# Attention stage: each step's reciprocals written 64 times by GpSimd and turned beside the last keys of the next step

## The chip, the cores and the metric

The kernel runs on one core of one Trainium2 chip. The metric is the device time of one execution in microseconds (us); less is better. TensorE (PE) multiplies matrices out of SBUF into PSUM, its weight loads are listed as PEld. VectorE (DVE) and ScalarE (ACT) work on SBUF and PSUM, GpSimd (POOL) on SBUF, and SyncE (SP) issues the DMAs. Each engine executes its own list in the order in which the program gave it; semaphores tie the lists together.

## The reference, cut to what matters

```python
scores = scale * q @ k.T + bias                # B=2, H=8, S=576, D=64; bias from a small MLP of positions
attn = np.exp(scores - scores.max(-1))
attn = attn / (attn.sum(-1) + 1e-9)
x = attn @ v                                   # -> (1152, 512)
# then 8 soft-gated experts:  out += P[:, e] * (relu(x @ w1[e]) @ w2[e])
# then a dense ELU feed-forward block of width 2048
```

Everything is float32. The change concerns the division by the row sums of `attn`.

## The kernel before

The attention stage takes roughly the first 180 us; then come the experts and the dense block, on TensorE almost without a break. Attention is cut into 40 steps. A step `s` is one pair of heads, one batch and one tile of query rows (128 rows, or 64 for the last tile of a head: `TROW`). `run_step(s)` walks through a string of letters, and each letter emits one part of the work. So the string fixes the order in which every engine meets its instructions. `ORD_S` holds for steps 0 to 2, `ORD_A` while bias rows are still being computed (up to step 13), `ORD_B` after that, `ORD_E` for the step after the last.

The letters that matter here, in step `s`:

- `R`, `S` (`emit_ttr`, L1265): for the first and the second head, DVE adds the bias to the scores in PSUM, writes them to SBUF and keeps the row minimum of their negative. In this document R of a step means the start of its first such instruction.
- `E`, `F` (`emit_exp`, L1280): ACT takes the exponentials and the row sums `sm`.
- `N` (`emit_norm`, L1288): POOL adds 1e-9 to the two row sums of step `s-1`, into `rc`.
- `Z` (`emit_recip`, L1292): DVE takes the reciprocal of `rc` in place; before the change for step `s-2`.
- `T`, `U` (`emit_tr`, L1308, L1315, L1406): PE turns the 128x512 exponentials of both heads of step `s-1`, in row halves of 64; ACT copies one half of the result to `aT` at once, DVE the other at `U`.
- `V` (`emit_trl`, L1332): the last 64 keys of both heads are turned in the same way; ACT (L1337) and DVE (L1335) copy a half of 64 columns each.
- `a` (`av_pieces`, L1355): one fifth of the product of `aT` with the values, for step `s-2`. With the fifth piece come the spreading products (L1367): two products of the broadcast `rc` with the identity, which put each row's reciprocal on the 64 partitions of its head, in the same PSUM bank as the result.
- `X` (`x_evac`): ACT copies the spread reciprocals to SBUF (`xf`, L1385), DVE multiplies the result by them (L1386) into `xt`. This frees the bank.
- `p` (`prep_next`, L1212, L1216): high and low parts of queries and keys; for the blocks prepared from step 13 on, DVE casts and POOL subtracts. `g` (`do_bg`): one part of the conversion of expert weights (`w_split`) or of `xt` (`ops_first`), POOL and ACT. `Q` (`emit_qk`, L1253): the scores of step `s+1`. `M`, `O`, `H`: the bias.

When these conversions fall due stands in two lists: `BG` starts one at steps 17, 22, 27 and 32, in five parts, one a step; `PS` starts the last three preparations at steps 16, 17 and 18.

PSUM: while the bias is computed the value products of all steps use one bank (`psC[0]`), afterwards two in turn.

Of the kernel before, what the change touches and what calls it, by code (L numbers as in the profile page):

```python
# [7 lines left out]
F32 = mybir.dt.float32  # L8
# [3 lines left out]
ACTF = mybir.ActivationFunctionType  # L12
ALU = mybir.AluOpType
# [17 lines left out]
LAG = 1  # L31
# [9 lines left out]
ACC = [2.6, 3.1]  # L41
WARM = 8
PS = [[1, 0], [2, 1], [3, 2], [4, 13], [5, 16], [6, 17], [7, 18]]
ORD_S = "RZMXTSOHUapaMEOHaaNpMFOHaLVQ"
ORD_A = "XRZOTSUapaMEaOHaNpaFLVMHQ"
ORD_B = "RZTSNXUaaLEaaappFVgQ"
ORD_E = "XZfTNVUaafaaa"
TOFF = [0, 128, 256, 384, 512]
TROW = [128, 128, 128, 128, 64]
NN = [256, 320]  # L50
# [184 lines left out]
def attention_moe_elu_ffn_kernel(  # L235
# [14 lines left out]
    act, dve, pe, pool, sp = nc.scalar, nc.vector, nc.tensor, nc.gpsimd, nc.sync  # L250

    def sb(name, bufs, st=ctx, side="left"):
        return st.enter_context(tc.tile_pool(name=name, bufs=bufs, side=side, reuse_waits="tile"))
# [13 lines left out]
    psB = psum("psB", 2, [128, 512])  # L267
    psC = [psum("psC", 1, [128, 512]), psum("psD", 1, [128, 512])]
# [5 lines left out]
    ident = csb[:, C_ID:C_ID + 128]  # L274
# [8 lines left out]
    xt = [new_xt(n) for n in range(NTILE)]  # L283
# [867 lines left out]
    steps = [(hp, b, t) for i, grp in enumerate(groups) for t in (TO if i == 0 else range(5)) for hp, b in grp]  # L1151
    gorder = [g for t in TO for g in range(8 * t, min(8 * t + 8, GRP))]
    NS = len(steps)
    right = ctx.enter_context(ExitStack())
    left = ctx.enter_context(ExitStack())

    def attention(fill):
# [2 lines left out]
        ep = sb("e", LAG + 2, right, "right")  # L1160
        atp = sb("attnT", AB, right, "right")
        tp = sb("tiny", 8, right, "right")
        xfp = sb("xf", LAG + 1, right, "right")
        bp = sb("bias", NB, left)
        up = sb("u", 1, left)
        ring = [xp.tile([128, 6, S], F32, tag=t, name="ring") for t in ("oh0", "ol0")]
# [5 lines left out]
        etile = {}  # L1172
# [6 lines left out]
        ev_q = []  # L1179
        scs = {}  # L1180
        rcs = {}

        def load_qk(i):
            hp, b = blocks[i]
# [103 lines left out]
            pool.tensor_scalar(rc[0:r], sm[0:r], EPS, None, ALU.add)  # L1288

        def emit_recip(s):  # L1290
            rc = rcs[s][0:TROW[steps[s][2]]]
            dve.reciprocal(rc, rc)  # L1292

        def emit_tr(s):
            r = TROW[steps[s][2]]
            et = etile[s][0]
            a = aT[s] = atp.tile([128, 9, 128], F32, tag="aT", name="aT")
            p = [psB("tr")]
            p.append(p[0] if r == 64 else psB("tr"))
            for jj in range(8):  # L1300
                c0 = 640 * (jj // 4) + 128 * (jj % 4)
                if r == 64:
                    parts = [(p[0], 64 * jj, 0)]
                else:
                    parts = [(p[0], 64 * jj, 0), (p[1], 64 * jj, 64)]
                for pt, c, o in parts:
                    q = slice(o, o + 64)
                    pe.transpose(pt[:, c:c + 64], et[q, c0:c0 + 128], ident[q, q], tile_position=(o, 0))  # L1308
            n = 4 if r == 64 else 8
            for k, pt in enumerate(p):  # L1310
                c0 = 256 * k if r == 64 else 0
                src = pt[:, c0:c0 + 64 * n].rearrange("p (j q) -> p j q", j=n)
                dst = a[:, 4 * k:4 * k + 4, 0:64] if r == 64 else a[:, 0:8, 64 * k:64 * k + 64]
                if k == 0:
                    act.activation(out=dst, in_=src, func=ACTF.Copy)  # L1315
                else:
                    at_q.append((dst, src))

        def emit_trl(s):
            r = TROW[steps[s][2]]  # L1320
            et = etile.pop(s)[0]
            if no[0] == GRP and 0 < s < NS - 2 and av_i[0] != s % 2:
                av_i[0] = s % 2
                av_b[s] = psC[s % 2]("av")
                parts = [(av_b[s], 256, 0)]
            else:
                parts = [(psB("trl"), 0, 0)]
            if r > 64:
                parts.append((av_p[0], 256, 64) if av_p[0] is not None else (psB("trl"), 0, 64))
            for pt, c, o in parts:  # L1330
                q = slice(o, o + 64)
                pe.transpose(pt[:, c:c + 64], et[q, 512:640], ident[q, q], tile_position=(o, 0))  # L1332
            for pt, c, o in parts:
                if o:
                    dve.tensor_copy(aT[s][:, 8, o:o + 64], pt[:, c:c + 64])  # L1335
                else:
                    act.activation(out=aT[s][:, 8, o:o + 64], in_=pt[:, c:c + 64], func=ACTF.Copy)  # L1337

        def av_pieces(s):
            hp, b, t = steps[s]  # L1340
            r = TROW[t]
            box = {}

            def piece(j):
                def f():
                    if j == 0:
                        if s not in av_b:
                            av_i[0] = 1 if s >= NS - 2 else s % 2 if no[0] == GRP else 0
                            av_b[s] = psC[av_i[0]]("av")
                        box["p"] = av_p[0] = av_b.pop(s)  # L1350
                    p = box["p"]
                    vt = vts[hp, b]
                    a = aT[s]
                    for h in range(2):
                        pe.matmul(  # L1355
                            p[64 * h:64 * h + 64, 0:r],
                            vt[:, j - 1 if j else 4, 64 * h:64 * h + 64],
                            a[:, 4 * h + j - 1 if j else 8, 0:r],
                            start=(j == 0),
                            stop=(j == 4),  # L1360
                            skip_group_check=True,
                        )
                    if j == 4:
                        n, o = XN[b][t], 64 * b if t == 4 else 0
                        rc = rcs.pop(s)
                        for h in range(2):
                            pe.matmul(  # L1367
                                p[64 * h:64 * h + 64, 128:128 + r],
                                rc[0:r, h:h + 1].to_broadcast([r, 64]),
                                ident[0:r, 0:r],  # L1370
                                start=True,
                                stop=True,
                                skip_group_check=True,
                            )
                        ev_q.append((p, r, hp, n, o))
                        aT.pop(s)
                return f

            return [piece(j) for j in range(5)]

        def x_evac():
            while ev_q:
                p, r, hp, n, o = ev_q.pop(0)
                xf = xfp.tile([128, 128], F32, tag="xf", name="xf")[:, 0:r]
                act.activation(out=xf, in_=p[:, 128:128 + r], func=ACTF.Copy)  # L1385
                dve.tensor_tensor(out=xt[n][:, hp, o:o + r], in0=p[:, 0:r], in1=xf, op=ALU.mult)  # L1386

        def av(n):
            for _ in range(min(n, len(av_q))):
# [8 lines left out]
        def run_step(s):  # L1398
            d = s - LAG
            cur, tr = s < NS, 0 <= d < NS  # L1400
            for x in ORD_S if s < 3 else ORD_A if no[0] < GRP else ORD_B if cur else ORD_E:
                if x == "T" and tr:
                    emit_tr(d)
                elif x == "U":
                    while at_q:
                        dve.tensor_copy(*at_q.pop(0))  # L1406
                elif x == "V" and tr:
                    emit_trl(d)
                elif x == "Q" and s + 1 < NS:
                    emit_qk(s + 1)  # L1410
                elif x in "RS" and cur:
                    emit_ttr(s, "RS".index(x))
                elif x in "EF" and cur:
                    emit_exp(s, "EF".index(x))
                elif x == "N":
                    if 1 <= s <= NS:
                        emit_norm(s - 1)
                elif x == "Z":
                    if 2 <= s:
                        emit_recip(s - 2)  # L1420
                elif x == "X":
                    x_evac()
                elif x == "a":
                    av(1)
                elif x == "M":
                    bias_p()
                elif x == "O":
                    bias_o()
                elif x == "H":
                    bias_hh()  # L1430
                elif x == "p":
                    for _ in range(3 if s < 4 else 1):
                        prep_next()
                elif x == "g":
                    do_bg(1)
                elif x == "L":
                    bias_loads(s)
                elif x == "f":
                    fill_pe(s)
            if tr:  # L1440
                av_q.extend(av_pieces(d))
# [137 lines left out]
        for s in range(NS + LAG):  # L1579
# [26 lines left out]
            if s == 15:  # L1606
                w = csb[:, C_WG:C_WG + 4 * E].rearrange("p (k e) -> p k e", k=4)
                dve.memset(wg32, 0.0)
                dve.tensor_copy(wg32[:, :, 0:E], w)
        emit_recip(NS - 1)  # L1610
        while av_q:
            x_evac()
            next(filler, None)
# [78 lines left out]
```

## Time and profile before

| | us |
|---|---|
| median of 3 runs | 1141.88 (1139.05 to 1143.20) |
| the profiled execution | 1138.75 |
| its span, first to last instruction | 1136.9 |

| engine | busy us in the span | share |
|---|---|---|
| PE | 1113.5 | 98% |
| PEld | 978.8 | 86% |
| DVE | 885.9 | 78% |
| ACT | 613.1 | 54% |
| POOL | 74.4 | 7% |

The mean granted TensorE clock was 0.994 of full speed. POOL's 74.4 us lie almost all between 98 and 170 us of the span. A timeline row gives the start in us, the length in us, engine, line, operation, the tile written and the tiles read, and in brackets how long the engine had been idle and what it waited for. A row of the chain of waits gives the start, the share of the time it accounts for, and the instruction.

### The profile page before, as it was taken

How to read it: one execution, taken by the hardware profiler on the slowest of the kernel's cores; microseconds unless marked ns; L12 is line 12 of the kernel's file. 1: busy time of each engine (PE TensorE's matmuls, PEld its weight loads, DVE VectorE, ACT ScalarE, POOL GpSimd, SP SyncE). 2: the span in 40 equal slices, each digit the busy share in tenths (PEclk: the TensorE clock that was granted, in tenths of full speed). 3: DMA queues.
4: the chain of work that ended last, by engine and by line, in shares of the span. 5: the costliest groups of instructions: out<-in, count | busy, mean ns of one | idle time of the engine just before them, and what ended most of it. 6: DMA issues, size and time to landing. Idle time of an engine off the chain costs nothing.

```text
span 1136.9 us, 20986 instructions
## 1 busy us (share of the span) xinstructions
PE 1113.5 (98%) x8122; PEld 978.8 (86%) x8122; DVE 885.9 (78%) x1903; ACT 613.1 (54%) x1417; POOL 74.4 (7%) x106
## 2 busy tenths in 40 slices
PE   7899999999999999999999999999999999999998
PEld 3467899989899999989898998989999887999896
DVE  7798887768877888878888788787666569888876
ACT  7998897543444444434444343434434366876663
POOL 0002750000000000000000000000000013000000
PEclk8899999999999999999999999999999999999999
DMA  6667530301232232322322323231111100021002
GB/s 200 212 216 249 176 86 20 112 20 38 84 112 93 93 113 65 112 95 92 112 82 100 109 73 112 93 106 53 55 55 39 56 20 19 20 75 37 22 17 84
DMA packets 36035, 100.16 MB, mean 88 GB/s; under 512 B 3808, under 2 KB 3936, under 8 KB 35936
## 3 DMA queue, kind: packets, MB, share of 16 engines
q1 hardware_dynamic: 35936, 98.82, 26.4%
q8 instruction: 64, 1.05, 0.4%
q14 instruction: 35, 0.29, 0.1%
HBM read 77.16 MB, written 21.64 MB: 87 GB/s over the span
## 4 chain that ended last, share of the span: by engine, by line
PE 90%; DVE 4%; ACT 3%; issue 1%; POOL 0%; ACTq 0%
PE y L751 42%; PE m L558 38%; PE av L1355 3%; PE sc L1253 2%; PE tr L1308 1%; PE bps L1492 1%; ACT ht L1474 1%; ACT et L1280 1%; DVE et L1265 1%; PE av L1367 1%; ACT o L1524 1%; PE av L1332 0%; DVE ol L457 0%; DVE c L662 0%; DVE a L658 0%
## 5 line engine op out<-in xcount | busy, mean ns | idle before, releaser
L558 PE MATMUL m<-oh,w1h 128*128 128x256 f32 (+1 forms) x1120 | 330.5, 295 | 0.9 <-ACT p L571 0.6
L558 PE MATMUL m<-ol,w1h 128*128 128x256 f32 (+1 forms) x1120 | 329.3, 294 | 0.1
L558 PE MATMUL m<-oh,w1l 128*128 128x256 f32 (+1 forms) x1120 | 329.0, 294 | 0.0
L751 PE MATMUL y<-w2h,hh 128*128 128x512 f32 x720 | 281.6, 391 | 0.7 <-ACT hh L665 0.6
L751 PE MATMUL y<-w2l,hh 128*128 128x512 f32 x720 | 281.5, 391 | 0.8 <-DVE w2l L457 0.8
L751 PE MATMUL y<-w2h,hl 128*128 128x512 f32 x720 | 281.6, 391 | 0.0
L558 PEld LDWEIGHTS m<-oh,w1h 128*128 128x128 f32 x1120 | 210.2, 188 | 7.4 <-ACT u L571 1.1
L558 PEld LDWEIGHTS m<-ol,w1h 128*128 128x128 f32 x1120 | 210.1, 188 | 5.6 <-DVE ol L457 0.5
L558 PEld LDWEIGHTS m<-oh,w1l 128*128 128x128 f32 x1120 | 210.4, 188 | 0.0
L571 ACT ACTIVATE u<-m 128x256 f32<-128x256 f32 (+1 forms) x160 | 65.3, 408 | 197.7 <-PE m L558 197.7
L751 PEld LDWEIGHTS y<-w2h,hl 128*128 128x128 f32 x720 | 135.2, 188 | 27.9 <-DVE hl L668 0.4
L751 PEld LDWEIGHTS y<-w2h,hh 128*128 128x128 f32 x720 | 135.2, 188 | 26.0 <-ACT hh L665 0.9
L751 PEld LDWEIGHTS y<-w2l,hh 128*128 128x128 f32 x720 | 135.2, 188 | 25.2 <-DVE w2l L457 1.1
L782 DVE SCALAR_TENSOR_TENSOR acc<-y,P,acc 128x512 f32<-128x512 f32 x126 | 94.5, 750 | 60.0 <-PE y L751 59.8
L621 ACT ACTIVATE hh<-c 128x512 fp32r<-128x512 f32 (+3 forms) x128 | 68.9, 558 | 60.4 <-DVE c L590 60.4
L624 DVE SCALAR_TENSOR_TENSOR hl<-c,hh 128x512 fp32r<-128x512 f32 (+3 forms) x128 | 77.6, 607 | 24.5 <-ACT hh L621 21.7
L571 ACT ACTIVATE p<-m 128x256 f32<-128x256 f32 (+1 forms) x160 | 65.5, 409 | 53.2 <-PE m L558 50.0
L1265 DVE CUSTOM_DVE_ANT_0 et<-sc,bt 128x576 f32<-128x576 f32 (+1 forms) x80 | 59.4, 745 | 17.4 <-PE sc L1253 15.5
L450 ACT ACTIVATE w2h<-raw 128x512 fp32r<-128x512 f32 x80 | 48.5, 627 | 40.8 <-PE y L751 40.0
L1280 ACT ACTIVATE et<-et,nmx 128x576 f32<-128x576 f32 (+1 forms) x80 | 61.7, 776 | 0.5 <-DVE nmx L1265 0.4
L457 DVE TENSOR_TENSOR w2l<-raw,w2h 128x512 fp32r<-128x512 f32 x80 | 53.8, 690 | 9.1 <-ACT w2h L450 9.1
L590 DVE TENSOR_TENSOR c<-u,p 128x256 f32<-128x256 f32 (+1 forms) x80 | 37.9, 473 | 25.1 <-ACT u L571 24.7
(139 smaller groups left out, 1495.9 us busy)
## 6 DMA issues: line engine op xcount, KB each, us to landing
raw<-w1p SPq DMA_DIRECT2D x32, 512.0 KB, 3.3
raw<-w2p SPq DMA_DIRECT2D x32, 512.0 KB, 3.3
scr<-o SPq DMA_DIRECT2D x36, 295.5 KB, 2.6
bt<-scr SPq DMA_DIRECT2D x16, 576.0 KB, 4.5
cw<-w1d SPq DMA_DIRECT2D x16, 512.0 KB, 4.0
wsc<-ca SPq DMA_DIRECT2D x32, 256.0 KB, 3.3
cw<-w2d SPq DMA_DIRECT2D x16, 512.0 KB, 4.0
raw<-wsc SPq DMA_DIRECT2D x16, 512.0 KB, 3.5
```

Source lines behind the costliest of these rows:

```text
L450: act.activation(out=dst(bh.get()), in_=src(), func=ACTF.Copy)
L457: lambda e: eng[e].tensor_tensor(out=dst(bl.get()), in0=src(), in1=dst(bh.get().bitcast(F32)), op=ALU.subtract),
L558: lambda e, w=w, o=o, j=j, k=k: pe.matmul(x["ap"](bank), w.get()[:, ai, j, :], o.get()[:, bi, j, :], start=(k == 0 and i in (1, 2, 5)), st ...
L571: lambda e: act.activation(out=b.get()[:, 0:N], in_=x["ap"](bank), func=ACTF.Copy),
L590: lambda e: eng[e].tensor_tensor(out=blk(b.get()[:, half * N:half * N + N], rev), in0=ap(p), in1=ap(q), op=ALU.add),
L621: op([("A", cA(w))], lambda e: act.activation(out=hh(), in_=ap(), func=ACTF.Relu), r=sk, w=wh, after=gate_)
L624: lambda e: dve.scalar_tensor_tensor(out=bl.get()[:, d], in0=ap(), scalar=0.0, in1=hhf(), op0=ALU.max, op1=ALU.subtract),
L751: lambda e, a=a, w=w, f=f, i=i, y=y, c=c: pe.matmul(y.get(), a.get()[:, c], w.get(), start=(f == 0 and i == 0), stop=(f == 3 and i == 2)),
L782: lambda e: dve.scalar_tensor_tensor(out=a.get(), in0=y.get(), scalar=P[0][:, n, e_:e_ + 1], in1=a.get(), op0=ALU.mult, op1=ALU.add),
L1265: dve.tensor_tensor_reduce(out=e.rearrange("p (x j) -> p x j", x=2), in0=sc[0:r, :, 0:HALF], in1=biast[hp, t][0:r, h].rearrange("p (x j) - ...
L1280: act.activation(out=e, in_=e, func=ACTF.Exp, scale=-1.0, bias=nmx[0:r, h:h + 1], accum_out=sm[0:r, h:h + 1])
L1355: pe.matmul(p[64 * h:64 * h + 64, 0:r], vt[:, j - 1 if j else 4, 64 * h:64 * h + 64], a[:, 4 * h + j - 1 if j else 8, 0:r], start=(j == 0) ...
```

## The change

POOL now writes each reciprocal 64 times into a new 128x128 tile `rb`, right behind DVE's reciprocal. `emit_trl(s)` turns `rb` of step `s-1` beside the last keys of step `s` with two more row-half transposes; ACT's and DVE's copies take both blocks, 128 columns instead of 64, into a tenth plane of `aT`. The multiplication reads that plane. The two spreading products and ACT's copy `xf` are gone. `N` stands first in each string, `Z` stands behind `U` and takes the reciprocal of step `s-1`, and `X` stands behind `R`. After the last step one more `emit_trl` turns the last `rb`.

```diff
-ORD_S = "RZMXTSOHUapaMEOHaaNpMFOHaLVQ"
-ORD_A = "XRZOTSUapaMEaOHaNpaFLVMHQ"
-ORD_B = "RZTSNXUaaLEaaappFVgQ"
-ORD_E = "XZfTNVUaafaaa"
+ORD_S = "NRMXTSOHUZapaMEOHaapMFOHaLVQ"
+ORD_A = "NRXOTSUZapaMEaOHapaFLVMHQ"
+ORD_B = "NRXTSUZaaLEaaappFVgQ"
+ORD_E = "XNfZTVUaafaaa"
...
         def emit_recip(s):
-            rc = rcs[s][0:TROW[steps[s][2]]]
+            r = TROW[steps[s][2]]
+            rc = rcs[s][0:r]
             dve.reciprocal(rc, rc)
+            rbs[s] = rbp.tile([128, 128], F32, tag="rb", name="rb")
+            pool.tensor_copy(rbs[s][0:r].rearrange("p (h d) -> p h d", h=2), rc.unsqueeze(2).to_broadcast([r, 2, 64]))
...
         def emit_trl(s):
+            z = s - 1
+            w = []
+            if s < NS:
+                w.append((8, TROW[steps[s][2]], etile.pop(s)[0][:, 512:640]))
+            if z >= 0:
+                w.append((9, TROW[steps[z][2]], rbs.pop(z)))
...
+            for k, r, src in w:
+                c = 64 * k - 256
+                for x in range(r // 64):
+                    q = slice(64 * x, 64 * x + 64)
+                    pe.transpose(halves[x][:, c:c + 64], src[q], ident[q, q], tile_position=(64 * x, 0))
...
-                        for h in range(2):
-                            pe.matmul(
-                                p[64 * h:64 * h + 64, 128:128 + r],
-                                rc[0:r, h:h + 1].to_broadcast([r, 64]),
-                                ident[0:r, 0:r],
...
-                xf = xfp.tile([128, 128], F32, tag="xf", name="xf")[:, 0:r]
-                act.activation(out=xf, in_=p[:, 128:128 + r], func=ACTF.Copy)
-                dve.tensor_tensor(out=xt[n][:, hp, o:o + r], in0=p[:, 0:r], in1=xf, op=ALU.mult)
+                dve.tensor_tensor(out=xt[n][:, hp, o:o + r], in0=p[:, 0:r], in1=aT[k][:, 9, 0:r], op=ALU.mult)
...
                 elif x == "Z":
-                    if 2 <= s:
-                        emit_recip(s - 2)
+                    if 1 <= s <= NS:
+                        emit_recip(s - 1)
```

## Rows read from the trace of the kernel before

**Rows 1.** Chain of waits: start us, us, what; one step mid-attention
```profile
138.75 1.24 PE av L1355 x20
139.99 0.22 PE av L1367 x4
140.21 0.21 PE av L1332 x2
...
141.26 0.49 PE tr L1308 x16
```

**Rows 2.** Timeline, DVE's six instructions in that step
```profile
138.29 0.76 DVE L1265 CUSTOM_DVE_ANT_0 et<-sc,bt 128x576 f32<-128x576 f32 x1 [0.57 <-PE sc L1253]
...
138.97 0.16 DVE L1292 RECIPROCAL rc<-rc 128x2 f32<-128x2 f32 x1
139.05 0.74 DVE L1265 CUSTOM_DVE_ANT_0 et<-sc,bt 128x576 f32<-128x576 f32 x1
...
139.71 0.29 DVE L1386 TENSOR_TENSOR xt<-av,xf 128x128 f32<-128x128 f32 x1
...
139.91 0.68 DVE L1406 COPY aT<-tr 128x512 f32<-128x512 f32 x1
...
140.51 0.21 DVE L1335 COPY aT<-av 128x64 f32<-128x64 f32 x1
```

**Rows 3.** Timeline of POOL, steps 17 to 23
```profile
109.66 1.43 POOL L1216 TENSOR_TENSOR ql<-ring,qh 128x576 fp32r<-128x576 f32 x1
...
115.44 0.30 POOL L1288 TENSOR_SCALAR rc<-sm 128x2 f32<-128x2 f32 x1
...
117.56 1.44 POOL L1216 TENSOR_TENSOR ql<-ring,qh 128x576 fp32r<-128x576 f32 x1
...
121.16 0.21 POOL L1288 TENSOR_SCALAR rc<-sm 128x2 f32<-128x2 f32 x1
...
123.36 1.43 POOL L1216 TENSOR_TENSOR ql<-ring,qh 128x576 fp32r<-128x576 f32 x1
...
127.51 0.21 POOL L1288 TENSOR_SCALAR rc<-sm 128x2 f32<-128x2 f32 x1
127.80 0.73 POOL L319 TENSOR_TENSOR st<-raw 128x256 f32<-128x256 f32 x1
...
130.81 0.21 POOL L1288 TENSOR_SCALAR rc<-sm 128x2 f32<-128x2 f32 x1
```

**Rows 4.** Timeline of DVE, steps 16 to 24: R of 17 and 24, casts
```profile
108.68 0.45 DVE L1212 CAST qh<-ring 128x576 fp32r<-128x576 f32 x1
...
109.42 0.22 DVE L1335 COPY aT<-av 128x64 f32<-128x64 f32 x1
109.55 0.75 DVE L1265 CUSTOM_DVE_ANT_0 et<-sc,bt 128x576 f32<-128x576 f32 x1
...
121.67 1.53 DVE L1212 CAST kh<-ring 128x576 fp32r<-128x576 f32 x1
...
132.27 0.76 DVE L1265 CUSTOM_DVE_ANT_0 et<-sc,bt 128x576 f32<-128x576 f32 x1 [0.56 <-PE sc L1253]
```

**Rows 5.** Timeline, a step in which the bias is still computed
```profile
89.41 0.29 DVE L1386 TENSOR_TENSOR xt<-av,xf 128x128 f32<-128x128 f32 x1
89.61 0.75 DVE L1265 CUSTOM_DVE_ANT_0 et<-sc,bt 128x576 f32<-128x576 f32 x1
...
90.00 0.66 PE L1355 MATMUL av<-aT,vt 128*64 128x128 f32 x8
```

**Rows 6.** Timeline, DVE and PE in step 14, the first in the order of `ORD_B`
```profile
100.41 0.29 DVE L1386 TENSOR_TENSOR xt<-av,xf 128x128 f32<-128x128 f32 x1
...
100.85 1.31 PE L1355 MATMUL av<-aT,vt 128*64 128x128 f32 x20 [1.35 <-DVE xt L1386]
```

**Rows 7.** Stretches: us; PE, PEld, DVE, ACT, POOL busy (x); granted clock, DMA share, GB/s
```profile
18.00:20.00 2.00, 1.13 (x16) 0.50 (x16) 0.15 (x2) 0.65 (x2) 0.00 (x0) 1.00 1.00 349
...
22.00:24.00 2.00, 0.99 (x18) 0.20 (x8) 2.00 (x6) 1.84 (x5) 0.00 (x0) 0.50 0.84 321
```

More of the change, by code (lines that the diff above doesn't have):

```diff
@@ L1162, in attention @@
         tp = sb("tiny", 8, right, "right")
-        xfp = sb("xf", LAG + 1, right, "right")
+        rbp = sb("rb", 2, right, "right")
         bp = sb("bias", NB, left)
@@ L1181, in attention @@
         rcs = {}
+        rbs = {}
         def load_qk(i):
@@ L1296, in emit_tr @@
             et = etile[s][0]
-            a = aT[s] = atp.tile([128, 9, 128], F32, tag="aT", name="aT")
+            a = aT[s] = atp.tile([128, 10, 128], F32, tag="aT", name="aT")
             p = [psB("tr")]
@@ L1319, in emit_trl @@
         def emit_trl(s):
-            r = TROW[steps[s][2]]
-            et = etile.pop(s)[0]
+            z = s - 1
[4 more added lines that the diff above has]
+                w.append((9, TROW[steps[z][2]], rbs.pop(z)))
             if no[0] == GRP and 0 < s < NS - 2 and av_i[0] != s % 2:
                 av_i[0] = s % 2
-                av_b[s] = psC[s % 2]("av")
-                parts = [(av_b[s], 256, 0)]
-            else:
[L1327 to L1335, printed above, removed]
+                halves = [psC[s % 2]("av")]
+                av_b[s] = halves[0]
+            else:
+                halves = [psB("trl")]
+            if max(r for _, r, _ in w) > 64:
+                halves.append(psB("trl") if av_p[0] is None else av_p[0])
+            for k, r, src in w:
[3 more added lines that the diff above has]
+                    pe.transpose(halves[x][:, c:c + 64], src[q], ident[q, q], tile_position=(64 * x, 0))
+            for x, p in enumerate(halves):
+                ks = [k for k, r, _ in w if r > 64 * x]
+                n = len(ks)
+                c = 64 * ks[0] - 256
+                dst = aT[s][:, ks[0]:ks[0] + n, 64 * x:64 * x + 64]
+                src = p[:, c:c + 64 * n].rearrange("p (k q) -> p k q", k=n)
+                if x:
+                    dve.tensor_copy(dst, src)
                 else:
-                    act.activation(out=aT[s][:, 8, o:o + 64], in_=pt[:, c:c + 64], func=ACTF.Copy)
+                    act.activation(out=dst, in_=src, func=ACTF.Copy)
         def av_pieces(s):
@@ L1364, in f @@
                         n, o = XN[b][t], 64 * b if t == 4 else 0
-                        rc = rcs.pop(s)
-                        for h in range(2):
-                            pe.matmul(
-                                p[64 * h:64 * h + 64, 128:128 + r],
-                                rc[0:r, h:h + 1].to_broadcast([r, 64]),
-                                ident[0:r, 0:r],
[L1371 to L1375, printed above, removed]
+                        ev_q.append((p, r, hp, n, o, s + 1))
                         aT.pop(s)
@@ L1382, in x_evac @@
             while ev_q:
-                p, r, hp, n, o = ev_q.pop(0)
-                xf = xfp.tile([128, 128], F32, tag="xf", name="xf")[:, 0:r]
-                act.activation(out=xf, in_=p[:, 128:128 + r], func=ACTF.Copy)
-                dve.tensor_tensor(out=xt[n][:, hp, o:o + r], in0=p[:, 0:r], in1=xf, op=ALU.mult)
+                p, r, hp, n, o, k = ev_q.pop(0)
+                dve.tensor_tensor(out=xt[n][:, hp, o:o + r], in0=p[:, 0:r], in1=aT[k][:, 9, 0:r], op=ALU.mult)
         def av(n):
@@ L1609, in attention @@
                 dve.tensor_copy(wg32[:, :, 0:E], w)
-        emit_recip(NS - 1)
+        aT[NS] = atp.tile([128, 10, 128], F32, tag="aT", name="aT")
+        emit_trl(NS)
         while av_q:
```

## The prediction

> **What bounds the kernel now.** I read the busy shares of the page first: PE is busy for 98% of the span, so what is worth something is what stands on PE's path. The change touches only the attention stage, so I read the chain of waits there, one step at a time. From about step 15 to step 36 the chain of a step is PE alone: the value products 1.24 us, the spreading products 0.22, the last keys 0.21, the scores (the row left out, 0.84 by difference), the transposes 0.49, together 3.00 us from one step to the next [rows 1]. The reader should see that no other engine appears. Then the timeline of DVE in the same step [rows 2]: it starts R when the scores are there and has waited 0.57 us for them, so DVE has about that much to spare per step. Last the timeline of POOL [rows 3], which no chain names: from 109.66 to 131 us it works without a break, and the little instruction that adds 1e-9 to the row sums stands in that list between long conversions.
>
> **The change, part by part**
>
> *PE.* The spreading products go: -0.22 us a step [rows 1]. Two more transposes come. Sixteen of the same form, in row-half pairs, take 0.49 us, so one pair is 0.06 us [rows 1]. Net -0.16 a step where PE is the bound; both ends for the unknown transposes are 0.03 (one more instruction) and 0.21 (a pair costs as much as the present pair of last keys). I take 0.06, the row with sixteen in sequence, since the new pair follows its like.
>
> *ACT and DVE copies.* ACT loses `xf`. Both copies get 64 columns more: 512 columns take 0.68 us and 64 take 0.21 [rows 2], so 0.07 for 64. DVE has 0.57 to spare and loses nothing here; ACT is relieved more than it is charged, and it isn't in the chain of these steps: 0.
>
> *The order on DVE.* From R of a step, by the distances in [rows 2]: the multiplication can start after 0.68, S 0.20 later, U 0.66 later, the reciprocal 0.60 later, so at R+2.14. The multiplication's input comes from the V of the step before, which lies before R: no new wait there.
>
> *POOL's copy.* No row shows it. It lies between the 1e-9 instruction (2 columns, 0.21 us) and what half of a 128x256 sum (0.73) would be, 0.21 + (0.73 - 0.21)/2 = 0.47 us [rows 3]. It reads one input where the sum reads two; I take 0.35, and 0.08 to the next instruction. It starts about 0.22 after the reciprocal starts (0.16 us long). So POOL can begin its conversions 0.65 us after DVE's reciprocal.
>
> *The wait that this makes.* Before, POOL went from the 1e-9 instruction straight to the conversions, which began at R+0.1 (109.66 against 109.55 [rows 3, 4]), and DVE took the reciprocal a step later. Now POOL waits for the reciprocal before it may convert, at R+2.14+0.65; the next 1e-9 instruction queues behind the conversions of the step; and DVE needs it in that same next step, at its R+2.14. What is queued behind the waiting reciprocal on DVE: the casts, the copy of the last keys, and R of the step after. For the copy PE's value products wait, and R holds the exponentials. So it is a loop: reciprocal, copy, conversions W, 1e-9 (0.25 us to its end), reciprocal. A step has 2.84 us (3.00 - 0.16); the loop needs 0.65 + W + 0.25. It binds when W is above about 1.95 us.
>
> W from [rows 3], first conversion to the next 1e-9 instruction: step 17, 109.66 to 115.44, 5.78; step 19, 117.56 to 121.16, 3.60; step 21, 123.36 to 127.51, 4.15; step 22, 127.80 to 130.81, 3.01. Steps 18, 20 and 23 hold a single subtraction (about 1.4, as the 128x576 one): not bound. With r for the start of the reciprocal, counted from R of step 17:
> r17 = 2.14; r18 = r17 + 0.65 + 5.78 + 0.25 = 8.82, where DVE would be ready at about 5.0.
> Behind it on DVE come two casts, 0.74 together (108.68 to 109.42 [rows 4]), 0.08 for the reciprocal and 0.20 for the copy (0.13 before [rows 4], plus 0.07), and then R of 19: 1.02, plus c for a cast that meets POOL. So r19 = r18 + 1.02 + c + 2.14 = 11.98 + c.
> r20 = r19 + 0.65 + 3.60 + 0.25 = 16.48 + c; casts again: r21 = r20 + 3.16 + c = 19.64 + 2c; r22 = r21 + 5.05 = 24.69 + 2c; r23 = r22 + 3.91 = 28.60 + 2c; R of 24 = r23 + 0.28 = 28.88 + 2c.
> Before, R of 24 came 132.27 - 109.55 = 22.72 after R of 17 [rows 4]. Loss: 6.16 + 2c.
>
> *c.* A cast of 0.45 us took 1.53 where POOL was in a long instruction [rows 4]: 1.1 lost. Now the casts come right behind the reciprocal, as POOL is about to run the short copy and then a subtraction of about 1.3. Ends: 0 (both casts get in first) and 1.6 (copy and subtraction are both waited out). I take 0.5, about half of what that row lost, because the first cast starts before POOL's copy: 2c = 1.0 and the loss 7.2 us. The Trainium skill, SBUF — State Buffer, section "SBUF: two separate sides", says that VectorE (in a two-port mode) and GpSimd lock the pair of ports that they share for a whole instruction and the loser fully blocks; by that rule alone c would be 1.6 and the sum 2.2 us higher, and the trace's 1.53 us cast agrees with whole-instruction blocking.
>
> *Steps 24 to 39.* Two later steps (28, 33) hold two sums and a subtraction, about 2.9 us by the same rows: the reciprocal then comes 3.8 after the one before, R two steps on at 2.14 + 3.8 + 0.28 = 6.2 in place of 5.7: +0.5 each, +1.0. All 16 steps from R of 24 gain 0.16: -2.6.
>
> *Before step 17.* In `ORD_A` the multiplication stood before R; now it stands behind it. All value products then share one PSUM bank, so PE can't start a step's value products before the multiplication has read the last. Before, it ran at 89.41, just ahead of R at 89.61, and PE went on at 90.00 [rows 5]. Now it would start at 89.61 + 0.68 and end 0.29 later, plus 0.15 to PE (its end to PE's start at step 14, 100.41 + 0.29 to 100.85 [rows 6]): 90.73. That is 0.7 us of waiting, less the 0.16: +0.55. PE is the whole chain in the last four such steps (10 to 13): +2.2. In the nine before them ACT and DVE are the longer ones and I take 0, between -0.15 and +0.2 each. In step 14 PE waited 1.35 us for the multiplication behind S [rows 6]; it now comes a reduction (0.74) earlier [rows 2]. With the -0.16 of steps 14 and 15: -1.1.
>
> *The end.* The last spreading is one more pair of transposes among the first expert products, in place of a product and a copy: 0.
>
> Sum: +7.2 + 1.0 - 2.6 + 2.2 - 1.1 = +6.7 us. The profiled execution took 1138.75 (span 1136.9 and 1.85 around it), so 1145.4; it lies 3.1 below the median of the runs. Against the median, 1141.88 + 6.7 = 1148.6. I take 1148.5.
>
> **The rivals**
>
> *The loop is hidden, the PE gain stands.* The place is DVE's wait at Z; it decides when PE has work left for as long as DVE waits. For it: DVE has 0.57 to spare and PE can turn the next exponentials meanwhile. Against it: 0.57 + 0.49 is short of the first wait, 8.82 - 5.0. Then every step from 17 on gains 0.16 (23, -3.7), and with +2.2 and -1.1 the sum is -2.6: 1139.3, not slower.
>
> *PE as the only bound, and early steps too.* If also the wait in steps 10 to 13 is covered (DVE early enough), -3.7 - 1.1 - 0.6 for these steps = -5.4, and with a reciprocal's worth of gap before the transposes gone (up to 0.17 in 20 steps) -8.8: 1136.5 to 1133. Against it is the same first wait.
>
> *The clock falls and the casts collide.* PE stands idle for 3.8 - 0.5 us at step 18 and shorter at 20, 22 and 23. Early in this kernel PE was busy for 1.13 of the 2 us from 18 on, at a granted clock of 1.00; from 22 on the clock is 0.50, the 1.2 GHz level [rows 7]. At that level a step's 2.84 us of PE work becomes 5.7. One such step hides behind the next wait; two that don't cost 2 x 2.84 = 5.7, half of which falls into waits: +3. With c at 1.6, +2.2 more: 1148.5 + 5 = 1153.5. The Trainium skill, TensorE: Matmul & The Clock Gate, section "What's actually happening", says that the low rate is the default and activity lifts it; by that rule the idle at step 18 would bring 1.2 GHz back, and the early stretches agree, with 0.50 behind a stretch in which PE was half idle.
>
> *The bias steps all pay.* If the 0.55 falls on the nine earlier steps too: +5, 1153.5.
>
> **How the numbers follow.** The loop as summed: 0.55, between 1144 (c = 0, POOL's copy 0.21, steps 10 to 13 half covered) and 1152. Hidden: 0.18. Faster on PE alone: 0.11. Clock and casts: 0.10. All bias steps: 0.06. No change that a measurement can tell is within 0.5%, 5.7 us, so up to 1147.6 and down to 1136.2. Of the first case somewhat over half lies above 1147.6 (0.32), the rest (0.23) below. Slower 0.32 + 0.16 = 0.48; same 0.23 + 0.17 = 0.40; faster 0.11 + 0.01 = 0.12. Range for 8 in 10: 1139 to 1154.5; the likeliest case alone 1144 to 1152.
>
> **What would show it.** In the trace after: DVE idle before the reciprocal in steps 18, 20, 22 and 23 with POOL as releaser, the first about 3.8 us; R of 17 to R of 24 near 30 us instead of 22.72; undisturbed steps at 2.84 instead of 3.00; PE idle about 0.6 before the value products of steps 10 to 13, released by the multiplication; POOL's copy near 0.35. The prediction is wrong if DVE never waits for POOL, if POOL's copy takes well under 0.2 or over 0.6 us, or if the step stays at 3.00.

## The result and the profile after

Over eight executions each, the kernel before took 1139.34 us in the median (1137.43 to 1143.20), the changed one 1147.02. One execution of the changed kernel took 1407.26 us at a granted clock of 0.724; it is left out of the ratio, and without it the median is 1146.45. The ratio is 1.006, with a 95% interval of 1.0036 to 1.0084: slower by about 6.8 us (4.1 to 9.6). The profiled execution took 1144.72 us (span 1142.9), 6.0 more than the profiled one of before (1138.75).

The best way to read it is by R, the start of a step's first reduction, in both traces. All stretches are differences of two such starts, in us:

| stretch | before | after | difference |
|---|---|---|---|
| R of 0 to R of 4 (start-up) | 29.59 | 28.00 | -1.6 |
| R of 4 to R of 14 (bias steps) | 49.53 | 54.09 | +4.6 |
| R of 14 to R of 17 | 10.56 | 9.75 | -0.8 |
| R of 17 to R of 24 (long conversions on POOL) | 22.72 | 28.83 | +6.1 |
| R of 24 to R of 39 | 45.10 | 42.73 | -2.4 |

With R of 0 at 20.04 against 19.87 (+0.17) that is +6.07 at R of 39, and the expert stage that follows adds nothing: the span is 6.0 longer.

The chain of waits of the changed kernel from the reciprocal in step 17 to the scores for step 20 (start, us, what) shows the loop. Here POOL, in no chain before, carries it:

```profile
114.03 0.16 DVE rc L1294
...
114.32 0.09 POOL rb L1296
...
114.58 1.42 POOL ql L1217
116.01 1.40 POOL kl L1217
117.40 0.70 POOL st L319
...
118.17 2.09 POOL st L319 x3
...
120.34 0.23 POOL rc L1289
...
120.59 0.17 DVE rc L1294
120.75 0.36 DVE qh L1213
121.11 0.46 DVE kh L1213
121.57 0.21 DVE aT L1350
...
121.91 2.40 PE av L1370 x20
124.32 0.41 PE av L1342 x3
124.72 1.59 PE sc L1254 x8
```

Read it from the top: the reciprocal of step 17, POOL's copy, the two subtractions and four sums, the 1e-9, the reciprocal of step 18, then casts, the copy of the last keys, and only then PE. In [rows 3] the conversions began at 109.66, 0.11 after R of 17; now they begin 2.7 us after R of 17 (111.88), and the 1e-9 (`rc` on POOL) ends 6 us after that.

DVE's timeline (start, us, engine, line, operation, tiles; in brackets the idle time before it and what ended it), with R of 17, the three longest waits and R of 24 (these answer to [rows 4]):

```profile
111.88 0.74 DVE L1266 CUSTOM_DVE_ANT_0 et<-sc,bt 128x576 f32<-128x576 f32 x1
...
120.59 0.17 DVE L1294 RECIPROCAL rc<-rc 128x2 f32<-128x2 f32 x1 [3.78 <-POOL rc L1289]
...
136.62 0.17 DVE L1294 RECIPROCAL rc<-rc 128x2 f32<-128x2 f32 x1 [2.13 <-POOL rc L1289]
...
140.44 0.17 DVE L1294 RECIPROCAL rc<-rc 128x2 f32<-128x2 f32 x1 [1.31 <-POOL rc L1289]
...
140.71 0.75 DVE L1266 CUSTOM_DVE_ANT_0 et<-sc,bt 128x576 f32<-128x576 f32 x1
```

The waits are those of steps 18, 22 and 23. The one forecast for step 20 is missing. The stretches show why (us; PE, PEld, DVE, ACT, POOL busy; granted clock, DMA share, GB/s):

```profile
118.00:120.00 2.00, 0.00 (x0) 0.00 (x0) 0.00 (x0) 0.60 (x1) 1.92 (x4) 0.97 0.26 102
120.00:122.00 2.00, 0.09 (x2) 0.12 (x4) 1.41 (x5) 0.00 (x0) 1.58 (x4) 0.50 0.00 0
122.00:124.00 2.00, 2.00 (x20) 1.92 (x20) 1.99 (x7) 1.47 (x3) 0.91 (x2) 0.50 0.00 0
124.00:126.00 2.00, 2.00 (x20) 1.75 (x18) 0.29 (x1) 1.01 (x4) 1.88 (x3) 0.50 0.25 51
126.00:128.00 2.00, 2.00 (x40) 1.92 (x36) 1.69 (x6) 0.90 (x2) 1.92 (x3) 0.82 1.01 394
```

While DVE waited, PE did nothing at all, and the clock went to 0.50, the 1.2 GHz level, for step 19 (121.69 to 126.31): its value products took 2.40 us instead of 1.24. The 0.82 is the mean of a stretch in which the clock rose again. But R of 20 could come late for free, up to a point: POOL's 1e-9 for step 20's reciprocal ended at 128.19 anyway, and the reciprocal ran at 128.47. So the slow clock cost about 0.3 us there.

An undisturbed step, in the chain:

```profile
146.79 1.24 PE av L1370 x20
148.03 0.27 PE av L1342 x4
148.30 0.85 PE sc L1254 x12
149.15 0.49 PE tr L1312 x16
```

Against [rows 1], 0.22 + 0.21 have become 0.27: four transposes in place of two and the products. The step is 2.85 instead of 3.00.

A bias step, in the chain (it answers to [rows 5]):

```profile
90.44 1.03 PE sc L1254 x12
...
91.50 0.51 issue
...
92.23 0.21 DVE xt L1389
92.44 0.14 issue
92.58 0.66 PE av L1370 x8
```

The scores end at 91.47, the value products begin at 92.58: 1.1 us, of which the transposes fill half. The rest is PE's wait for the multiplication, now behind R. In the kernel before, ACT and DVE carry most of the chain in the bias steps ahead of step 9; in step 6 it is ACT's list:

```profile
60.15 0.75 ACT et L1280 x2
60.90 0.90 ACT ht L1474 x2
61.81 0.76 ACT et L1280 x2
```

In the changed kernel every bias step from step 6 on has the chain shown for [rows 5]: PE's products, R, the multiplication, PE again.

### The profile page after: what moved, and what is told of

It reads as the page before. It is cut to its first block, busy times and chain, and to the rows that moved or that the text cites. A ratio compares the mean times of both kernels' runs of the same rounds, so it can differ in the third digit from the quotient of the medians.

```text
span 1142.9 us, 20811 instructions
## 1 busy us (share of the span) xinstructions
PE 1107.9 (97%) x8034; PEld 974.8 (85%) x8034; DVE 887.2 (78%) x1904; ACT 611.0 (53%) x1378; POOL 91.8 (8%) x146
## 4 chain that ended last, share of the span: by engine, by line
PE 88%; DVE 4%; ACT 2%; issue 1%; POOL 1%; DVEq 0%; POOLq 0%; ACTq 0%
PE y L751 42%; PE m L558 38%; PE av L1370 3%; PE sc L1254 2%; PE bps L1495 2%; PE tr L1312 1%; DVE et L1266 1%; ACT et L1281 0%; DVE ol L457 0%; ACT o L1527 0%; POOL ql L1217 0%; POOL kl L1217 0%; PE av L1342 0%; DVE c L662 0%; POOL st L356 0%
## 5 line engine op out<-in xcount | busy, mean ns | idle before, releaser
L624 DVE SCALAR_TENSOR_TENSOR hl<-c,hh 128x512 fp32r<-128x512 f32 (+3 forms) x128 | 77.6, 607 | 24.6 <-ACT hh L621 21.8
L1370 PE MATMUL av<-aT,vt 128*64 128x128 f32 (+1 forms) x800 | 52.8, 273 | 13.4 <-DVE xt L1389 7.8
L1370 PEld LDWEIGHTS av<-aT,vt 128*64 128x64 f32 x800 | 41.3, 139 | 25.7 <-issue 13.5
```

Source lines behind the costliest of these rows:

```text
L624: lambda e: dve.scalar_tensor_tensor(out=bl.get()[:, d], in0=ap(), scalar=0.0, in1=hhf(), op0=ALU.max, op1=ALU.subtract),
L1370: pe.matmul(p[64 * h:64 * h + 64, 0:r], vt[:, j - 1 if j else 4, 64 * h:64 * h + 64], a[:, 4 * h + j - 1 if j else 8, 0:r], start=(j == 0) ...
```

## The experiments

Medians are of the runs made together; each ratio is against the kernel before, run on the same chip.

| run | R 4 to 14 | R 17 to 24 | R 24 to 36 | median | ratio (95%) |
|---|---|---|---|---|---|
| kernel before | 49.53 | 22.72 | 36.27 | | |
| changed kernel | 54.09 | 28.83 | 34.45 | 1147.02 | 1.006 (1.0036 to 1.0084) |
| e4: X behind R in the kernel before | 54.59 | 22.71 | 36.23 | 1144.29 | 1.0045 (1.0031 to 1.0059) |
| e2: X before R in the changed kernel | 48.60 | 28.60 | 34.45 | 1140.10 | 1.0012 (1.0003 to 1.0022) |
| e1: 1e-9 on DVE | 54.35 | 25.16 | 34.29 | 1142.66 | 1.0037 (1.0022 to 1.0051) |
| e3: 1e-9 and copy on DVE | 52.54 | 25.39 | 35.95 | 1142.82 | 1.0031 (1.0017 to 1.0045) |
| e5: POOL's copy twice | 54.10 | 30.05 | 35.17 | 1150.59 | 1.0095 (1.0068 to 1.0122) |
| e6: early reciprocal in the kernel before | 49.55 | 24.55 | 36.15 | 1141.33 | 1.0012 (0.9998 to 1.0025) |
| e8: late reciprocal, copy on POOL | 48.36 | 25.72 | 34.24 | 1136.87 | 0.9986 (0.9971 to 1.0001) |
| e7: late reciprocal, copy on ACT | 49.09 | 21.78 | 34.69 | 1136.33 | 0.9974 (0.9959 to 0.9989) |
| e9: as e7, copy first in the step | 49.79 | 21.63 | 34.15 | 1134.39 | 0.9963 (0.9948 to 0.9978) |

The stretch from R of 0 to R of 4 is left out of the table: it took 27.4 to 34.1 us in these traces, and the granted clock between 18 and 50 us was 1.00 in the first of these and 0.68 in the last. So R of 14 as such, a figure in six of the expectations, moves with the start-up; the stretch from 4 to 14 is what the edits change.

**e4 and e2: the order of X.**

```diff
 e4, on the kernel before:
-ORD_A = "XRZOTSUapaMEaOHaNpaFLVMHQ"
+ORD_A = "RXZOTSUapaMEaOHaNpaFLVMHQ"
 e2, on the changed kernel:
-ORD_A = "NRXOTSUZapaMEaOHapaFLVMHQ"
+ORD_A = "NXROTSUZapaMEaOHapaFLVMHQ"
```

> The kernel before with one edit: in the order of the bias steps the multiplication X stands behind R (RXZOT... for XRZOT...). Theory: PE waits in these steps for the multiplication, R of 14 comes 2.5 to 4 us later than the 98.99 of the kernel before, everything after it is unchanged, the total rises by about 3 us (ratio about 1.0026). Rival (the order alone costs nothing; the wait in the changed kernel comes from its other parts): R of 14 within 0.5 us of 98.99 and the same total.

> The changed kernel with one edit: in the order of the bias steps the multiplication X stands before R again (NXROT... for NRXOT...). Theory (PE waits there for the one bank of the value products): PE no longer waits for the multiplication in steps 3 to 13, R of 14 comes at 98.5 to 99.5 us instead of 102.1, R of 17 to R of 24 stays 28 to 29 us, the total falls by about 3 us against the changed kernel. Rival (the bias steps are longer because of the wider copies and of POOL's copy): R of 14 stays between 101.5 and 102.5 and the total stays.

e4 alone costs 5.06 us from R of 4 to R of 14 and nothing behind: 22.71 and 36.23 are the figures of before. It was more than expected, and it is the order and nothing else, since nothing else differs. PE's timeline in e4 names the wait (the releaser is put down as the reciprocal that stands next on DVE):

```profile
88.74 0.66 PE L1355 MATMUL av<-aT,vt 128*64 128x128 f32 x8 [0.66 <-DVE rc L1292]
```

e2 gives 5.5 us back in the same stretch, again more than the 3 forecast, and leaves the loop at 28.60. Its total is 0.5% below the changed kernel's. The rival is out in both. So the order costs 5.1 to 5.5 us here, and the other parts of the change give back 0.5 to 0.9 of it (e2 lies 0.93 below the kernel before).

**e1 and e3: POOL's small instructions on DVE.**

```diff
 e1:
-            pool.tensor_scalar(rc[0:r], sm[0:r], EPS, None, ALU.add)
+            dve.tensor_scalar(rc[0:r], sm[0:r], EPS, None, ALU.add)
 ... and N directly ahead of Z in the strings; e3 also:
-            pool.tensor_copy(rbs[s][0:r]...
+            dve.tensor_copy(rbs[s][0:r]...
 ... and X before R in ORD_A
```

> The changed kernel with one edit: the instruction that adds 1e-9 runs on DVE just ahead of the reciprocal, instead of on POOL. Theory (DVE waits at the reciprocal because the 1e-9 instruction queues behind POOL's conversions, which themselves wait for the reciprocal): DVE never waits for POOL any more; POOL's copy of the reciprocals still stands behind the conversions, so PE waits once, about 1.5 us, for the last-key transposes of step 19; R of 17 to R of 24 falls from 28.83 us to about 22; R of 14 stays near 102; the total falls by 6 to 7 us against the changed kernel, to about the time of the kernel before. Rival (it is POOL's and DVE's use of the same memory ports, or POOL's added work as such, that costs the 6 us): the copies and the conversions are all still there, R of 17 to R of 24 stays above 27 us and the total does not fall by more than 1 us.

> The changed kernel with X before R in the bias steps, and both the 1e-9 and the 64-fold copy of the reciprocals on DVE, so that POOL is in no loop. Theory: DVE has about 0.5 us to spare in a step and pays about 0.3 for the two instructions; no engine waits for POOL except for the conversions; R of 14 near 99, R of 17 to R of 24 20.5 to 21.5 us, steps from 24 on 2.84 us, the total 4 to 6 us below the kernel before (ratio about 0.995 to 0.9965). Rival (DVE becomes the bound of a step): steps of 3.0 us or more and the total within 1 us of the kernel before.

e1 lies between the two: 3.7 us less from 17 to 24 where the theory said 6.8, and a total that fell by 0.2% where it said 0.5 to 0.6. DVE waits for no semaphore of POOL any more, but DVE's timeline at step 18 shows another wait in its place:

```profile
123.32 0.69 DVE L1409 COPY aT<-tr 128x512 f32<-128x512 f32 x1
123.92 0.92 DVE L1289 TENSOR_SCALAR rc<-sm 128x2 f32<-128x2 f32 x1
124.87 0.17 DVE L1294 RECIPROCAL rc<-rc 128x2 f32<-128x2 f32 x1
124.95 0.86 DVE L1213 CAST qh<-ring 128x576 fp32r<-128x576 f32 x1
```

The 1e-9 on two columns takes 0.92 us, to 124.84. POOL's timeline at the same time:

```profile
123.37 1.44 POOL L1217 TENSOR_TENSOR kl<-ring,kh 128x576 fp32r<-128x576 f32 x1
124.77 0.73 POOL L319 TENSOR_TENSOR st<-raw 128x256 f32<-128x256 f32 x1
```

The subtraction ended at 124.81, 0.03 us ahead of the 1e-9. In e3, in a step with POOL busy and in one with POOL idle:

```profile
117.20 1.09 DVE L1289 TENSOR_SCALAR rc<-sm 128x2 f32<-128x2 f32 x1
118.33 0.17 DVE L1294 RECIPROCAL rc<-rc 128x2 f32<-128x2 f32 x1
...
125.22 0.15 DVE L1289 TENSOR_SCALAR rc<-sm 128x2 f32<-128x2 f32 x1
```

POOL's subtraction ran from 116.99 to 118.27 in the first case, and the 1e-9 ended at 118.29. The Trainium skill, SBUF — State Buffer, section "SBUF: two separate sides", says that DVE in a two-port mode and POOL lock the port pair that they share for a whole instruction: the one that starts first has it, the other blocks. The trace agrees in both cases: the 1e-9 starts while the subtraction runs and ends right after it. A reciprocal of the same shape is not held up: e1's took 0.17 us at 124.87, with POOL's sum running from 124.77 (in e3 POOL stood idle at 118.33, so that row says nothing on it). So these two kernels traded a wait in the list for a wait at the port. The 2.4 us that are left of the 6.1 in e1 don't save its rival: e7 below keeps all casts and conversions and takes 21.78. e3's expectation failed altogether: its steps from 24 to 36 are 2.88 us at best, DVE's own length, and two of them over 3.5; from R of 4 to R of 14 it takes 52.54 where e2, with the same order, takes 48.60. Its rival has the bound right (DVE), but not the figures: most of its steps are under 3.0, and the total is 0.31% above the kernel before.

**e5: the copy twice.**

```diff
             pool.tensor_copy(rbs[s][0:r].rearrange("p (h d) -> p h d", h=2), rc.unsqueeze(2).to_broadcast([r, 2, 64]))
+            pool.tensor_copy(rbs[s][0:r].rearrange("p (h d) -> p h d", h=2), rc.unsqueeze(2).to_broadcast([r, 2, 64]))
```

> The changed kernel with POOL's copy of the reciprocals made twice. Theory (a loop of reciprocal, copy, conversions, 1e-9, reciprocal binds in the steps with long conversions, and POOL's time costs nothing elsewhere): one more copy of 0.26 to 0.33 us is paid in full at the reciprocals of steps 18, 22 and 23, and of 29 and 34, R of 17 to R of 24 rises by 0.8 to 1.3 us (from 28.83), steps such as 26 to 28 stay at 2.85, the total rises by 1 to 2 us. Rival (POOL's copy costs time in every step, through ports or latency): every step gets 0.2 to 0.3 us longer, the total rises by 8 us or more. Second rival (POOL is not in the path): no change.

R of 17 to R of 24 rose by 1.22 us, steps 26 to 28 were 2.84, 2.87 and 2.84, and 24 to 36 rose by 0.7. DVE's waits at the reciprocals of steps 18, 22, 23, 29 and 34 grew by 0.36 or 0.37 each, for the second copy (0.29) and the gap behind it. So more time on POOL counts where the loop binds and nowhere else. A wait of 0.40 shows at step 15 too, which neither the prediction nor this expectation names. The total rose by 0.35%, more than these 1.9 us, but from four executions and with overlapping intervals (1.0068 to 1.0122 and 1.0036 to 1.0084); in the profiled execution 3.5 us of it lie in the start-up, at a clock of 0.73. The total is no test here, the steps are.

**e6: only the early reciprocal.**

```diff
-ORD_B = "RZTSNXUaaLEaaappFVgQ"
+ORD_B = "NRTSXUZaaLEaaappFVgQ"
 ... ORD_S, ORD_A, ORD_E in the same sense, X kept first in ORD_A
-                        emit_recip(s - 2)
+                        emit_recip(s - 1)
```

> The kernel before (spreading products, ACT's copy, X before R in the bias steps and behind S later), with only the place of the reciprocal as in the changed kernel: the 1e-9 first in a step, the reciprocal of step s-1 behind U. POOL's conversions do not wait for the reciprocal here. Theory (the large wait needs both: the reciprocal a step sooner, and the conversions held back until it is done): one wait for POOL of about 1 us at step 18 and none at 20, 22, 23; R of 17 to R of 24 is 23 to 24.5 us, the total within 2 us of the kernel before. Rival (taking the reciprocal a step sooner is the whole of the wait): R of 17 to R of 24 near 28 us, the total 5 us or more above the kernel before.

DVE waits for POOL's 1e-9 once, as these two lines of its timeline at step 18 show, and the cast behind it runs into a long subtraction:

```profile
113.86 0.17 DVE L1292 RECIPROCAL rc<-rc 128x2 f32<-128x2 f32 x1 [1.02 <-POOL rc L1288]
113.94 1.54 DVE L1212 CAST qh<-ring 128x576 fp32r<-128x576 f32 x1
```

POOL's subtraction stood there from 113.91 to 115.17. The stretch takes 24.55, at the upper end of what was expected (24.5): 1.8 us against the 6.1 of the changed kernel. So the large wait needs the conversions to be held back as well. That is the copy's place in POOL's list.

**e8 and e7: the reciprocal late again.** Both turn the reciprocals as the changed kernel does, but take the reciprocal of step `s-2` first in a step, so about a step later than the change does. e8 leaves the copy on POOL, e7 puts it on ACT.

```diff
-ORD_B = "NRXTSUZaaLEaaappFVgQ"
+ORD_B = "ZRXTYSNUaaLEaaappFVgQ"
 ... ORD_A = "ZXROTYSUapaMEaOHaNpaFLVMHQ"; Z: emit_recip(s - 2); Y: emit_rb(s - 2), in e7 with
+            act.activation(
+                out=rbs[s][0:r].rearrange("p (h d) -> p h d", h=2), in_=rc.unsqueeze(2).to_broadcast([r, 2, 64]), func=ACTF.Copy
+            )
```

> As the run with the late reciprocal and the copy on ACT, but the 64-fold copy stays on POOL, behind the conversions of the step before. Theory (POOL's list in order is what costs: whatever a step needs of POOL soon stands behind the conversions): DVE no longer waits for the 1e-9, but PE waits for the copy at the last-key transposes of steps 18, 21 to 23, about 4 us together; R of 17 to R of 24 24 to 26 us; R of 14 near 96.6; the total 1 to 3 us below the kernel before. Rival (only the early reciprocal matters): as with the copy on ACT, R of 17 to R of 24 21 to 22 us.

> The changed kernel's transposes and read-out, but with the reciprocal of step s-2 first in a step as a step later, the 64-fold copy on ACT where its copy xf used to stand, the 1e-9 on POOL with a step to spare, and X before R in the bias steps (behind R later). Theory (the products on PE are worth 0.16 us a step, and the losses come only from POOL's loop and from the order of X): no wait of DVE or PE for POOL except a preparation; R of 14 near 96.6 us, R of 17 to R of 24 21 to 22 us, steps from 24 on 2.85 us, the total 5 to 7 us below the kernel before (ratio 0.994 to 0.996). Rival (ACT becomes the bound with the copy): steps of 2.9 to 3.0 us from 24 on and a total 2 to 4 us below.

In e8 the wait moved from DVE to PE, as its timeline has it:

```profile
116.55 0.37 PE L1346 MATMUL av<-csb,rb 64*128 64x64 f32 x2 [2.60 <-POOL rb L1300]
...
130.32 0.27 PE L1346 MATMUL av<-csb,rb 64*128 64x64 f32 x2 [0.57 <-POOL rb L1300]
133.84 0.28 PE L1346 MATMUL av<-csb,rb 64*128 64x64 f32 x2 [0.46 <-POOL rb L1300]
```

That is 3.6 us of waiting where about 4 were expected; the total (0.9986) can't be told from that of the kernel before.

In e7 the wait of 3.78 is gone: 21.78, inside its range. But "no wait of DVE or PE for POOL" was wrong. Two waits stay on DVE:

```profile
125.58 0.17 DVE L1294 RECIPROCAL rc<-rc 128x2 f32<-128x2 f32 x1 [0.63 <-POOL rc L1289]
...
128.90 0.17 DVE L1294 RECIPROCAL rc<-rc 128x2 f32<-128x2 f32 x1 [0.82 <-POOL rc L1289]
```

They are no loop: POOL's conversions here wait for nobody. POOL works from 107.07 to 128.87 with no gap of over 0.1 us, and R of 24 (129.02) comes right behind the reciprocal that waited for its 1e-9. So with the loop open, the stretch is about as long as POOL's list itself, 21.8 us for seven steps that would take 19.9 at 2.85; no run shortens that list. That the steps are worth 0.16 us each on PE is seen only in part behind that, because its steps are 2.91. The figures of the rival came true there: steps of 2.9 to 3.0 us and a total 2.8 us below. With the copy between ACT's copy of the turned exponentials and the exponentials, ACT's chain was thought to set the step; e9 tests that. The total missed the range of the theory (0.9974 against 0.994 to 0.996).

**e9: the copy first on ACT.** Y directly behind Z in all strings.

> As the run with the late reciprocal and the copy on ACT, but the copy is the first that ACT meets in a step, ahead of its copy of the turned exponentials, instead of between that copy and the exponentials. Theory (with the copy in between, a step is the chain transposes, ACT's copy, rb, two exponentials, 2.91 us; ACT waits about 0.45 us ahead of its copy of the turned exponentials where no conversion stands there): steps from 24 on without a conversion on ACT 2.84 to 2.87 us, R of 24 to R of 36 falls from 34.69 to 34.0 to 34.4 us, the total falls by 0.3 to 1 us. Rival (ACT is full in these steps wherever the copy stands): 34.6 to 34.8 us as before.

Steps 26 to 36 are 2.81 to 2.87, 24 to 36 takes 34.15 for 34.69: so the place of the copy on ACT set e7's steps of 2.91. DVE's two waits for POOL stay (0.65 and 0.82). This kernel has the lowest ratio of all, 0.37% below the kernel before and about 1% below the changed one; its total can't be told from e7's, since the intervals overlap.

## Why the prediction was right, point by point

The sum was +6.7 us, the measured ratio is +6.8 (4.1 to 9.6). The mechanism was the forecast one; that the sum agrees so closely is partly luck, since the parts were not all of the right size and their errors cancel. The 1148.5 as a time also rests on a median of three executions, 2.5 us above that of the eight.

- *PE.* -0.16 a step, a pair of transposes at 0.06: measured 3.00 to 2.85, and 0.27 for two pairs. Right. But "PE alone" from step 15 to step 36 was misread: in the kernel before, the chain of steps 18 and 20 runs through DVE's reductions and casts (0.94 and 1.53 us where 0.45 is undisturbed [rows 4]), and these steps take 3.59 and 4.18. The sum isn't touched, since it starts from the measured 22.72.
- *The wait.* R of 24 was put at 28.88 + 2c after R of 17, the first wait at 3.8. Measured 28.83 and 3.78. e6, e5 and e7 show each link: the early reciprocal alone 1.0 us of waiting, POOL's copy paid in full inside the loop, 21.78 when the loop is opened, with 0.63 and 0.82 us of waiting left. POOL's copy took 0.29, the estimate was 0.35 with bounds of 0.21 and 0.47.
- *c.* Taken at 0.5, measured 0.08 at both places: the two casts together took 0.82 where 0.74 is undisturbed. They come right behind the reciprocal, so they get in ahead of POOL, whose next subtractions took 1.47 and 1.49 instead of 1.29. The term was too large by 0.8. The 1.6 was reckoned as if POOL came first; the first cast started at 120.67, POOL's copy at 120.89. Waiting out a whole instruction is real (e1, e3); that POOL was the one held up here is read from the two lengths, and no run tests it.
- *Steps 24 to 39.* -1.6 forecast, -2.4 measured. The two later waits exist (0.64 and 0.63 us on DVE, at steps 29 and 34) but cost 0.15 and 0.08 instead of 0.5 each, since the step behind each was shorter, 2.70 and 2.64 for an undisturbed 2.85. The forecast counts 16 steps, the stretch holds 15.
- *The bias steps.* The mechanism was right, and e4 shows it by itself. The size was not: the wait was charged to four steps, because only there is PE the whole chain, and it is paid in all ten from 4 to 13, 0.17 to 0.72 us in each: +4.6 for +2.2. The four steps 10 to 13 pay 2.4, near the 2.2 of the forecast; the six before them, taken at 0, pay 2.1. The chains show why: a wait of 0.6 us makes PE the longest in the steps in which ACT and DVE had been. That was the rival in which all bias steps pay, and it belonged in the sum.
- *Steps 14 to 16.* -1.1 forecast, -0.8 measured. The prediction looked for the loop from step 17 on only. The preparation of step 14 makes W 2.90 (104.83 to 107.73), above its own limit of 1.95, and the chain runs through POOL there too; the reciprocal of step 15 comes 0.1 late, and 0.40 in e5.
- *The clock.* It fell as that rival said, for one step, and cost about 0.3 us, since the next wait for POOL covered it. The low rate as the state that activity lifts, the rule of the Trainium skill (TensorE: Matmul & The Clock Gate, section "What's actually happening"), agrees with the rows: 0.50 is granted from 120 on, behind 2 us in which PE did nothing, and 0.82 in the mean from 126 to 128, with PE busy again since 122. The rival's price for it, +3, was too high.
- *Start-up.* Nothing was forecast; -1.6 in the profiled execution. It goes with the granted clock there and differs by up to 6.7 us between traces. Why it differs from one execution to the next was not tried.

So the errors nearly cancel: measured less forecast is +2.4 in the bias steps, +0.3 in steps 14 to 16, -1.1 from R of 17 to R of 24 (6.1 for 7.2, most of it the casts), -0.8 behind it and -1.6 in the start-up, in all -0.8; with the 0.17 by which R of 0 came later, the profiled execution is 0.6 below the sum. The terms that failed are the 0 taken for the earlier bias steps (+2.1 measured in six of them) and c (0.08 for 0.5 at each of two places).

## What to carry to other kernels

An idle engine isn't a free one: what counts is what stands in its list ahead of the instruction that someone will wait for, and whether its long work is itself held back by that someone. When a short instruction is moved to such an engine, write down the loop (who releases whom, in which step) and compare it with the length of a step. Then compare the whole of that engine's list with the steps in which it must be done: with the loop open (e7), the stretch was about as long as that list. If a wait is added to an engine that is second in a step by less than the wait, charge it there too.

## What the runs showed of the hardware

A DVE `TENSOR_SCALAR` on two float32 columns in SBUF, 0.15 us when POOL is idle, took 0.92 (e1) and 1.09 us (e3) beside a POOL subtraction; `RECIPROCAL` on two columns took 0.17 beside a POOL sum (e1, at 124.87). POOL's copy of two columns, each repeated 64 times, to 128 columns took 0.29 us, less than half of its 128x256 sum (0.73).
